# A sparse attention and expert layer on one core: block sums on TensorE, key maxima ahead of the transposes, query copies in a row, a new order and 152 filler matmuls

## Chip, cores and metric

The kernel runs on one core of a Trainium2 chip. The time is the device time of one execution in microseconds. Before the change it was 207.64 us, the median of three runs (206.0 to 210.47).

## What is computed

Two stages, for batch 4, 8 heads, 768 tokens and head size 64. Stage 1 is attention in which each query sees a window of local keys and, for each block of 32 tokens, one maximum key and one mean value. Stage 2 is a mixture of four attention experts on the result.

```python
k_sum = k.reshape(B, H, nb, block, D).max(axis=3)      # block = 32, nb = 24
v_sum = v.reshape(B, H, nb, block, D).mean(axis=3)
mask_l = np.abs(pos[:, None] - pos[None, :]) < window  # window = 16
scores_l = scale * q @ k.T ; scores_s = scale * q @ k_sum.T + np.log(block)
a = softmax(concat([where(mask_l, scores_l, -1e9), scores_s]))
attn = a @ concat([v, v_sum])
# stage 2, x = attn as (B, S, H*D): for each of 4 experts
logits = x @ w_gate                                    # top 2 of 4, softmax w
a = softmax(where(causal, -1e9, scale * (x @ wq[e]) @ (x @ wk[e]).T))
out += mask * w * (a @ (x @ wv[e]) @ wo[e])
```

## The kernel before

The program is a list of steps. `make_plan` creates them, each with the buffers that it reads and writes, and `TABLE`, a text of some 730 words, gives the order in which they are emitted, the engine of each (V is VectorE or DVE, A ScalarE or ACT, G GpSimd or POOL, S SyncE or SP, P TensorE or PE) and the slots of its new buffers. Nothing is scheduled while it runs: on each engine instructions stand in the table's order, and one that waits holds up all behind it. Transfers are issued by POOL (keys and queries) and SP (all others), in order as well.

Heads are worked in pairs, four pairs for each of four batches; two pairs share one load of keys and queries. For a pair, stage 1 (`stage1_pair`) does this:

- `dv` (L268) loads V as 24 windows of 96 tokens and 64 features into `vb`; column 64 holds constants, for the softmax sums.
- `load_vs` (L235) loads V of two pairs a second time, 24 blocks of each head on 96 partitions, and adds the 32 tokens of each block in halves, in place, in five steps `tr` (L247) on POOL or DVE. `dsum` (L286) spreads the block sums by DMA into partitions 96 to 119 of `vb`, twelve copies for each head.
- `tk` (L296) transposes keys on PE, `ck` copies them to `kT`, `rk` (L305) takes block maxima from `kT`, and `kwc` and `ksc` (copies, L163 and L161 on their engines) set up `kw`, the windows with 24 maxima behind each.
- `tq` (L334) transposes the queries, with 128 partitions and 6 tokens on each. `cq` (L338) copies them out of PSUM to `qT`: in odd batches it writes in a row and reads with a stride, in even batches it reads in a row and writes with a stride.
- `scs` (L361 masks, L368 products) makes scores, `ex` (L375) their exponentials, `avs` (L385) the PV products in f32, `rc` and `xm` (L396, L400) normalize, `tx` (L410) transposes back, and `hic` and `loc` (L421) split the result into two f16 parts, `hi` and `lo`.

Stage 2 of a batch needs all four pairs of it: `pps` (L558) projects queries and keys of two experts, `vps` (L493, L496) makes values and gate logits, `sps` (L582) scores, `exs` (L590) exponentials, `dgm` (L595) the causal mask on the diagonal, `av2` (L606) products, then weights (L620, L624), a transpose (L633), the output product (L647), a copy and a store (L657). The table interleaves stage 2 of a batch with stage 1 of the next. All helper copies of DVE and POOL have line L163, those of ACT L161.

Of the kernel before, what the change touches and what calls it, by code (L numbers as in the profile page):

```python
# [50 lines left out]
19,S,0 4,G, 5,V, 20,V, 17,G,0 88,P,0.0 6,G, 21,V, 8,G, 22,V, 68,P,1.1 0,G,1 18,G,0 89,V, 91,A,0 73,P,0.0 3,G,1  # L51
69,V, 70,V,0 71,A,1 93,P,1.1 1,G, 72,A, 90,V,1 48,P,2.0 74,A, 94,A, 7,G, 77,P,4.0 78,A, 92,V, 23,G, 24,G,
95,P,0.1 75,P,6.2 76,A, 49,V, 51,V,2 50,V,1 52,V, 67,S,0 25,G,1 97,P,2.3 98,A, 66,S, 80,P,4.0.0 2,G, 53,P,6.2
54,V, 79,P, 28,P,2.1 9,S,1 81,V, 15,G, 96,A, 82,V, 33,P,3.0 29,V, 83,P,0.0.0 84,A, 57,P,4.4 58,A, 31,V,1
55,P,6.5 56,A, 213,G,2 283,P,2.0 30,V,0 32,A, 284,A, 87,S,2 86,S, 99,P,4.1.1 34,V, 35,P,2.0 36,A, 214,G,2
288,P,6.1 205,G,0 26,S, 10,G, 11,G, 85,V, 289,A, 37,P,0.2 12,G, 13,G, 14,G, 286,V,0 27,S, 100,P, 285,V,1
287,V, 101,V, 102,V, 223,P,2.1 224,V, 243,P,3.0 268,P,6.2 269,V, 292,P,4.1 38,A, 226,A,2 103,P,0.1.1 104,A,
244,V, 245,V,0 633,G,3 225,V,1 293,A, 227,V, 290,P,6.3 40,P,2.0.0 291,A, 105,V, 206,G,0 247,A,1 248,P,4.0
# [721 lines left out]
```

## Time and profile before

| | |
|---|---|
| median of three runs | 207.64 us |
| the profiled execution | 208.41 us |
| its span, first to last instruction | 206.4 us |
| PE, DVE, ACT, POOL busy | 149.7, 131.6, 123.1, 82.8 us |
| bytes moved | 33.17 MB, 161 GB/s on the mean |
| SP: V for `vb`, V for `vs`, sums to `vb` | 16, 8 and 32 loads |

The span is cut by its stages rather than read as a whole. The first 27.3 us are the start. From 27.3 to 61.6 stage 1 of batch 0 is finished and that of batch 1 begun. From 61.6, where the first expert projection starts, both stages run beside each other. What follows 195.3 us is the end of the last batch. A PE that is busy here is not at its peak: records of matmuls overlap, so what a step takes is read from its start to the next start.

### The profile page before, as it was taken

The page shows a single profiled execution, that of the slowest core. Times are in us where ns is not written, and L with a number is a line of the kernel's source. Part 1 is how long each engine was busy: PE and PEld are TensorE (multiplying, and loading weights), DVE is VectorE, ACT ScalarE, POOL GpSimd, SP SyncE. Part 2 cuts the span into 40 slices and gives each one's busy share as a digit, 9 for nine tenths or more (in the row PEclk, how much of TensorE's full clock was granted, in tenths as well). Part 3 has the DMA queues.
Part 4 walks back from the last instruction along what each step waited for, and adds up shares of the span by engine and source line. Part 5 has one row for each costly group of instructions (what it writes and reads, how often), then busy time and mean ns, then how long its engine had stood idle before and what let it go on. Part 6 is the DMA issues. An engine that isn't in the chain of part 4 may idle for free.

```text
span 206.4 us, 6279 instructions
## 1 busy us (share of the span) xinstructions
PE 149.7 (73%) x2704; PEld 115.2 (56%) x2704; DVE 131.6 (64%) x227; ACT 123.1 (60%) x152; POOL 82.8 (40%) x146
## 2 busy tenths in 40 slices
PE   0252277897369974737977978766999999999960
PEld 0242175686356753637754567655768767767620
DVE  0653029987666467604839998967498687636940
ACT  2199402658265854517997777344646888698740
POOL 7980009304520634236553954918722012223300
PEclk9999999999969999988999999999699999999997
DMA  6999999699999999999167997999698580200456
GB/s 154 187 150 187 223 175 148 80 183 208 167 199 230 168 163 183 204 210 246 24 105 128 219 184 113 219 260 265 105 175 166 139 137 17 89 3 0 165 194 254
DMA packets 65499, 33.17 MB, mean 161 GB/s; under 512 B 54208, under 2 KB 61376, under 8 KB 64704
## 3 DMA queue, kind: packets, MB, share of 16 engines
q1 hardware_dynamic: 58016, 26.48, 67.4%
q0 software_dynamic: 7456, 6.29, 20.2%
q8 instruction: 21, 0.34, 0.7%
q14 instruction: 6, 0.05, 0.1%
HBM read 30.41 MB, written 6.29 MB: 178 GB/s over the span
## 4 chain that ended last, share of the span: by engine, by line
PE 41%; DVE 21%; DMA 17%; issue 10%; ACT 6%; SPq 1%; POOL 1%; DVEq 0%; POOLq 0%; ACTq 0%
PE ps L385 9%; PE ps L558 7%; DMA vb<-in_v_dram 7%; DMA vb<-vs 7%; DVE qT L163 4%; PE ps L410 4%; PE ps L493 4%; PE ps L647 4%; PE ps L582 3%; DMA kn<-in_k_dram 3%; DVE ks L305 3%; PE ps L334 2%; PE ps L606 2%; PE ps L296 2%; DVE x L400 2%
## 5 line engine op out<-in xcount | busy, mean ns | idle before, releaser
L590 ACT ACTIVATE a<-ps 128x1024 f16<-128x1024 f32 (+1 forms) x48 | 42.0, 915 | 14.1 <-PE ps L582 12.6
L385 PE MATMUL ps<-vb,aT 120*64 120x65 f32 x768 | 30.1, 241 | 14.7 <-DMA vb<-in_v_dram 7.1
L595 POOL TENSOR_SCALAR_AFFINE_SELECT a<-a 128x256 f16<-128x256 f16 x48 | 18.9, 410 | 54.4 <-ACT a L590 49.6
L247 POOL TENSOR_TENSOR vs<-vs 96x1024 f32<-96x1024 f32 (+4 forms) x23 | 25.3, 1100 | 31.4 <-DMA vs<-in_v_dram 20.7
L385 PEld LDWEIGHTS ps<-vb,aT 120*64 120x64 f32 x768 | 27.8, 154 | 17.5 <-issue 11.9
L375 ACT ACTIVATE aT<-ps 120x768 f32<-120x768 f32 x32 | 25.2, 819 | 14.2 <-PE ps L368 11.3
L558 PE MATMUL ps<-hi,wqk 128*128 128x384 f16 x128 | 22.6, 326 | 1.6 <-ACT aT L375 1.6
L163 DVE COPY qT<-ps 128x768 f16<-128x768 f16 x6 | 12.9, 2145 | 12.4 <-PE ps L334 12.2
L163 POOL COPY kw<-kT 128x960 f16<-128x960 f16 (+1 forms) x14 | 15.7, 1153 | 11.6 <-PE ps L368 8.1
L410 PE MATMUL ps<-id,x 128*128 128x128 f32 x96 | 16.8, 320 | 4.5 <-issue 1.6
L421 DVE TENSOR_TENSOR lo<-ps,hi 128x768 f16<-128x768 f32 x16 | 15.4, 971 | 5.2 <-ACT hi L161 5.0
L361 PE MATMUL ps<-pi,mt 64*128 64x64 f16 (+1 forms) x128 | 12.8, 271 | 7.0 <-issue 3.3
L558 PEld LDWEIGHTS <-wqk 128*128 128x128 f16 x128 | 12.1, 98 | 9.4 <-issue 1.9
L296 PE MATMUL ps<-id,kn 96*64 96x96 f16 x256 | 10.1, 244 | 9.1 <-DMA kn<-in_k_dram 8.7
L410 PEld LDWEIGHTS ps<-id,x 128*128 128x128 f32 x96 | 12.7, 162 | 6.6 <-issue 2.1
L247 DVE TENSOR_TENSOR vs<-vs 96x512 f32<-96x512 f32 (+4 forms) x17 | 10.5, 615 | 8.9 <-DMA vs<-in_v_dram 7.0
L582 PE MATMUL ps<-qk,qk 64*128 64x512 f16 (+3 forms) x128 | 14.6, 307 | 2.1 <-DVE x L400 1.2
L368 PE MATMUL ps<-qT,kw 64*128 64x64 f16 x384 | 12.8, 204 | 4.2 <-ACT qT L161 2.3
L400 DVE TENSOR_TENSOR x<-ps,rec 128x768 f32<-128x768 f32 x16 | 15.3, 957 | 0.6
L161 ACT COPY qT<-ps 128x768 f16<-128x768 f16 x10 | 15.6, 1612 | 0.1
L161 ACT CAST hi<-ps 128x768 f16<-128x768 f32 x9 | 7.4, 825 | 13.5 <-PE ps L410 13.4
L305 DVE TENSOR_REDUCE ks<-kT 128x24 f16<-128x768 f16 x16 | 14.9, 944 | 0.1
(81 smaller groups left out, 260.8 us busy)
## 6 DMA issues: line engine op xcount, KB each, us to landing
vb<-in_v_dram SPq DMA_DIRECT2D x14, 576.0 KB
vs<-in_v_dram SPq DMA_DIRECT2D x8, 768.0 KB
out_dram<-ob SPq DMA_DIRECT2D x12, 512.0 KB
kn<-in_k_dram POOLq DMA_DIRECT2D x7, 384.0 KB, 6.9
qn<-in_q_dram POOLq DMA_DIRECT2D x7, 384.0 KB, 7.6
vb<-vs SPq DMA_DIRECT2D x32, 72.0 KB
vb<-in_v_dram SPq DMA_DIRECT2D x2, 552.0 KB
a<-in_moe_wq_dram SPq DMA_DIRECT2D x4, 128.0 KB
```

What stands on the lines that cost most here:

```text
L161: nc.scalar.copy(dst, src)
L163: en(e).tensor_copy(dst, src)
L247: en(e).tensor_tensor(w[:, 0:half], w[:, 0:half], w[:, half:2 * half], AL.add)
L305: nc.vector.tensor_reduce(T["ks"][ks.slot], T["kT"][kT.slot].rearrange("c (s n p) -> c n s p", s=8, n=NSUM), AX.XY, AL.max)
L375: nc.scalar.activation(T["aT"][aT.slot][0:KR], pbank(sc, 2)[0:KR, :, 0:384], AF.Exp, scale=SCALE)
L385: nc.tensor.matmul(pbank(av, 2)[o:o + 64, u, 65 * (2 * (t // 2) + hp):65 * (2 * (t // 2) + hp) + 65], a[0:KR, hp, 64 * t:64 * t + 64], T[" ...
L400: nc.vector.tensor_tensor(T["x32"][x32.slot].rearrange("p (u t w) -> p u t w", u=2, w=64), avv()[:, :, :, 0:64], T["rec"][rec.slot].to_bro ...
L410: nc.tensor.transpose(pbank(xp, 2)[:, t // 3, 128 * (t % 3):128 * (t % 3) + 128], T["x32"][x32.slot][:, 128 * t:128 * t + 128], T["id32"])
L558: nc.tensor.matmul(pbank(pp, 2)[:, u, 0:384], T["wqk"][:, ch, cc, j, :], hi_(ch)[:, 384 * u:384 * u + 384], start=(ch == 0), stop=(ch == N ...
L582: nc.tensor.matmul(pbank(sp, 2)[:, ep, c0:c0 + w], T["qk"][qk[1].slot][r, 128 * tj:128 * tj + 128], T["qk"][qk[0].slot][r, n0:n0 + w], sta ...
L590: nc.scalar.activation(a2v(u), pbank(sp, 2)[:, :, 0:ln], AF.Exp, scale=SCALE / (XS * XS))
L595: nc.gpsimd.affine_select(m, m, [[0, 2], [1, 128]], AL.is_ge, 0.0, base=0, channel_multiplier=-1)
```

## The change

- **Block sums.** `load_vs`, its adds and the spread by DMA are gone. `load_v` loads V into `vb` as before. `sums` multiplies what lies there with a matrix of zeros and ones, `sel`: 12 windows of a head add up in one bank of PSUM, each head in its own 32 partitions. A first copy (`be`) brings that to `vs`, now 24 partitions of 4 x 64 elements, and a second (`ds`), on POOL, DVE or ACT, spreads it into `vb`. In batch 0 a step does one pair, later two. `vb` has six slots instead of four.
- **Key maxima.** Loaded keys have 8 tokens on each of 96 partitions. Three DVE steps (`km`) take the maximum of these 8 from the loaded keys (512 to 256, 128, 64 columns a head); `tk` transposes that too, and `rk` reduces 4 columns instead of 32.
- **Queries** are loaded on 96 partitions with 8 tokens on each, as the keys are, and `cq` always writes in a row.
- **Weights.** `wqk` is two buffers, one for two experts each, so that each has its own copy. `av2` lists more exponentials among the buffers that its later parts read.
- **Fills.** 74, 28, 23, 13 and 14 matmuls of the identity with itself, 128 x 128, stand at five places ahead of the first PV products (`f` in the table).
- **Order.** The whole table is new.

```diff
-SLOTS = dict(qn=3, kn=3, kT=2, ks=2, kw=3, qT=3, aT=6, x32=2, vb=4, vs=2,
+SLOTS = dict(qn=3, kn=3, km=3, kT=2, ks=3, kw=3, qT=3, aT=6, x32=2, vb=6, vs=2,
-19,S,0 4,G, 5,V, 20,V, 17,G,0 88,P,0.0 6,G, 21,V, 8,G, 22,V, 68,P,1.1 0,G,1 18,G,0 89,V, 91,A,0 73,P,0.0 3,G,1
+116,S,0 27,G,0 28,G,0 29,V,0 30,V, 31,V, 10,G, f,P,7.74 76,P,0.0.0 12,V, 5,G,1 77,A, 94,P,1.1.1 99,P,2.0 78,V,
...
+    def sels(e):
+        z = T["sel"]
+        en(e).memset(z, 0.0)
+        nc.gpsimd.memset(z[:, 22:24], 1.0)
+        nc.gpsimd.affine_select(z[:, 22:24], z[:, 22:24], [[-32, 2]], AL.is_ge, 0.0,
+                                base=-16, channel_multiplier=1)
+        nc.gpsimd.affine_select(z[:, 22:24], z[:, 22:24], [[32, 2]], AL.is_ge, 0.0,
+                                base=47, channel_multiplier=-1)
...
+            for w in (256, 128, 64):
+                def mx(e, w=w, i=i):
+                    hs = slice(n * i, n * i + n)
+                    m = T["km"][km[b, g].slot][:, hs, :]
+                    x = T["kn"][kn[b, g].slot][:, hs, :] if w == 256 else m
+                    en(e).tensor_tensor(m[:, :, 0:w], x[:, :, 0:w], x[:, :, w:2 * w], AL.max)
...
-            def add(e, half=half):
-                w = T["vs"][t.slot]
-                en(e).tensor_tensor(w[:, 0:half], w[:, 0:half], w[:, half:2 * half], AL.add)
...
-                nc.sync.dma_start(out=w[WIN:KR, 12 * hp:12 * hp + 12, 0:64],
-                                  in_=s[r0:r0 + NSUM, 0:64].unsqueeze(1).to_broadcast((NSUM, NQ, 64)))
...
+    def sums(b, cs):
+        sp, t = R.buf("ps"), R.buf("vs")
+        def mm(e):
+            n = 2 * len(cs)
+            for tt in range(NQ):
+                for j in range(n):
+                    nc.tensor.matmul(pbank(sp)[32 * j:32 * j + 32, 0, 0:64],
+                                     T["sel"][:, 22 - 2 * tt:54 - 2 * tt],
+                                     T["vb"][vb[b, cs[j // 2]].slot][0:WIN, 12 * (j % 2) + tt, 0:64],
+                                     start=(tt == 0), stop=(tt == NQ - 1))
...
+        def ev(e):
+            for j in range(2 * len(cs)):
+                copy(e, T["vs"][t.slot][96:120, j, :], pbank(sp)[32 * j:32 * j + NSUM, 0, 0:64])
...
+                copy(e, T["vb"][vb[b, c].slot][WIN:KR, :, 0:64].rearrange("n (h t) d -> n h t d", h=2),
+                     T["vs"][t.slot][WIN:KR, 2 * i:2 * i + 2, :].unsqueeze(2).to_broadcast(
+                         (NSUM, 2, NQ, 64)))
...
+            for hp in range(2):
+                nc.tensor.transpose(pbank16(kp)[64 * hp:64 * hp + 64, 768:864],
+                                    T["km"][km[b, g].slot][:, hh + hp, 0:64], T["id16"][0:96, 0:96])
...
-                                    T["kT"][kT.slot].rearrange("c (s n p) -> c n s p", s=8, n=NSUM),
-                                    AX.XY, AL.max)
+                                    pbank16(kp)[:, 768:864].rearrange("c (n p) -> c n p", p=4),
+                                    AX.X, AL.max)
...
-            if b % 2:
-                copy(e, dst.rearrange("c (p s) -> c p s", s=6),
-                     src.rearrange("c (s p) -> c p s", s=6))
-            else:
-                copy(e, dst.rearrange("c (p s) -> c s p", s=6),
-                     src.rearrange("c (s p) -> c s p", s=6))
+            copy(e, T["qT"][qT.slot].rearrange("c (p s) -> c p s", s=8),
+                 pbank16(qp)[:, 0:S].rearrange("c (s p) -> c p s", s=8))
...
+    def fill(bank, n):
+        for _ in range(n):
+            nc.tensor.matmul(T["ps"][:, bank, 0:128], T["id16"], T["id16"], start=True, stop=True)
```

Two places show the new order. The first is SP's queue at the start. Before, it stood so (`vs` is V for the adds, `vb` the windows; L286 is the spread of sums):

```order
L240 DMA vs_100<-in_v_dram 96x2048
L286 DMA vb_96<-vs_100 24x12x64 x2
L268 DMA vb_96<-in_v_dram 96x24x64
L240 DMA vs_101<-in_v_dram 96x2048
L286 DMA vb_98<-vs_100 24x12x64 x2
L268 DMA vb_98<-in_v_dram 96x24x64
L262 DMA vb_97<-in_v_dram 80x64
L268 DMA vb_97<-in_v_dram 96x23x64
```

Now it begins with a weight (`a_136`), and the four pairs of V of batch 0 follow each other:

```order
L466 DMA a_136<-in_moe_wq_dram 128x4x64
L275 DMA vb_101<-in_v_dram 80x64
L281 DMA vb_101<-in_v_dram 96x23x64
L281 DMA vb_102<-in_v_dram 96x24x64
L281 DMA vb_103<-in_v_dram 96x24x64
L281 DMA vb_104<-in_v_dram 96x24x64
```

V of the first pairs no longer stands behind a spread that waits for adds. The second place is DVE ahead of its first normalization. Before, `pi`, adds (`vs`), key copies, maxima (`ks` from `kT`) and a query copy came there, of which these are the last:

```order
L163 COPY kT_78<-ps 128x768
L163 COPY kw_84<-kT_78 128x10x96
L163 COPY kw_84<-kT_78 128x2x80
L305 TENSOR_REDUCE ks_81<-kT_78 128x24
L163 COPY kw_84<-ks_81 128x12x24
L163 COPY qT_87<-ps 128x6x128
L396 RECIPROCAL rec_102<-ps 128x12
L400 TENSOR_TENSOR x_94<-ps,rec_102 128x768
```

Now the stretch from the key copy of pair 0 to the first normalization reads, with the sums (`vs_107`), two spreads into `vb` and the maxima of the next keys (`km_77`):

```order
L167 COPY kw_87<-kT_83 128x10x96
L167 COPY kw_87<-kT_83 128x2x80
L333 TENSOR_REDUCE ks_84<-ps 128x24
L167 COPY kw_87<-ks_84 128x12x24
L167 COPY vs_107<-ps 24x64 x2
L167 COPY vb_101<-vs_107 24x24x64
L167 COPY vb_102<-vs_108 24x24x64
L251 TENSOR_TENSOR km_77<-kn_81 96x1024
L251 TENSOR_TENSOR km_77<-km_77 96x4x128
L251 TENSOR_TENSOR km_77<-km_77 96x4x64
L419 RECIPROCAL rec_109<-ps 128x12
```

The query copies have moved from here to ACT, and the spreads and the next maxima stand ahead of the first normalization.

## Rows read from the trace of the kernel before

**Rows 1.** The page, section 2: PE's busy tenths in 40 equal slices.

```profile
PE   0252277897369974737977978766999999999960
```

**Rows 2.** Busy time of each engine in four stretches (us), TensorE's granted clock, DMA.

```profile
0.00:27.30 27.30, 6.89 (x138) 5.58 (x138) 9.03 (x15) 13.95 (x12) 12.82 (x44) 1.00 1.05 181
27.30:61.60 34.30, 25.48 (x528) 22.59 (x529) 26.35 (x34) 16.39 (x22) 13.03 (x14) 0.95 1.07 165
61.60:150.60 89.00, 69.09 (x1305) 53.06 (x1305) 60.07 (x105) 56.02 (x71) 46.72 (x62) 0.96 1.03 178
150.60:195.30 44.70, 44.52 (x714) 32.20 (x713) 32.87 (x71) 33.74 (x45) 10.23 (x27) 1.00 0.42 93
```

**Rows 3.** The chain that ended last: start us, us, what.

```profile
1.54 6.66 DMA kn<-in_k_dram
...
13.12 14.03 DMA vb<-in_v_dram
...
27.28 1.57 PE ps L385 x24
```

**Rows 4.** PE's waits from 61.6 to 150.6: us in total, times, longest.

```profile
PE ps L385 <- DMA vb<-vs: 6.9, 3, 4.2
...
PE ps L334 <- DVE qT L163: 1.5, 1, 1.5
PE ps L385 <- DMA vb<-in_v_dram: 1.5, 1, 1.5
```

**Rows 5.** Groups by line and shape: busy us, mean ns, idle before.

```profile
L385 PEld LDWEIGHTS ps<-vb,aT 120*64 120x64 f32 x768 | 27.8, 154 | 17.5 <-issue 11.9 <-DVE gt L536 2.7 <-ACT qk L161 2.2
...
L421 DVE TENSOR_TENSOR lo<-ps,hi 128x768 f16<-128x768 f32 x16 | 15.4, 971 | 5.2 <-ACT hi L161 5.0
L400 DVE TENSOR_TENSOR x<-ps,rec 128x768 f32<-128x768 f32 x16 | 15.3, 957 | 0.6
L305 DVE TENSOR_REDUCE ks<-kT 128x24 f16<-128x768 f16 x16 | 14.9, 944 | 0.1
L247 POOL TENSOR_TENSOR vs<-vs 96x1024 f32<-96x1024 f32 x6 | 14.1, 2356 | 30.3 <-DMA vs<-in_v_dram 20.7 <-issue 9.6
...
L163 POOL COPY kw<-kT 128x960 f16<-128x960 f16 x7 | 12.9, 1839 | 11.6 <-PE ps L368 8.1 <-ACT kT L161 3.5
...
L163 DVE COPY kT<-ps 128x768 f16<-128x768 f16 x11 | 6.2, 560 | 2.0 <-ACT kw L161 2.0
...
L163 DVE COPY kw<-kT 128x960 f16<-128x960 f16 x5 | 5.2, 1043 | 0.1
...
L247 DVE TENSOR_TENSOR vs<-vs 96x1024 f32<-96x1024 f32 x2 | 2.4, 1222 | 7.0 <-DMA vs<-in_v_dram 7.0
...
L163 DVE COPY kw<-kT 128x160 f16<-128x160 f16 x5 | 2.0, 392 | 0.0
...
L204 POOL MEMSET vb<- 128x24 f32 x4 | 0.6, 144 | 0.2
```

**Rows 6.** The start in order of time: start us, us, instructions.

```profile
5.06 1.49 POOL L227 DMA_DIRECT2D qn<-in_q_dram  x2
...
11.52 1.49 PE L334 MATMUL ps<-id,qn 128*64 128x128 f16 x24 [1.79 <-DMA qn<-in_q_dram]
```

**Rows 7.** PE in order of time, from the dense stretch.

```profile
163.92 1.62 PE L385 MATMUL ps<-vb,aT 120*64 120x65 f32 x48
165.37 0.51 PE L334 MATMUL ps<-id,qn 128*64 128x128 f16 x12
```

**Rows 8.** Busy time in two stretches with a lower clock; columns as in rows 2.

```profile
90.00:96.00 6.00, 5.09 (x110) 5.03 (x111) 2.08 (x4) 1.56 (x2) 1.48 (x1) 0.72 1.15 228
144.00:150.00 6.00, 5.73 (x86) 4.49 (x79) 2.48 (x4) 3.88 (x6) 4.61 (x5) 0.72 0.70 113
```

**Rows 9.** Query copies one by one: duration ns min/median/max, first and last start.

```profile
L161 ACT COPY qT<-ps x10: 798/835/2921, 14.3 to 165.9; 128x768 f16<-128x768 f16 x10
L163 DVE COPY qT<-ps x6: 942/2726/2775, 29.6 to 130.2; 128x768 f16<-128x768 f16 x6
```

More of the change, by code (lines that the diff above doesn't have):

```diff
@@ L133, in emit @@
         for i, eng, slots in table:
+            if i < 0:
+                self.fill(*slots)
+                continue
             st = self.steps[i]
@@ L281, in dsum @@
-        def dsum(e):
-            w = T["vb"][vb.slot]
-            s = T["vs"][vs[b, g].slot]
-            for hp in range(2):
-                r0 = NSUM * (hh + hp)
-                nc.sync.dma_start(out=w[WIN:KR, 12 * hp:12 * hp + 12, 0:64],
-                                  in_=s[r0:r0 + NSUM, 0:64].unsqueeze(1).to_broadcast((NSUM, NQ, 64)))
-        R.step(f"ds{b}{c}", {"S": 0.9}, [vs[b, g], vones], [vb], dsum, dma=2 * 288 * 0.017 / 16)
+        if edge:
+            R.step(f"zv{b}{c}", {"V": 0.1, "G": 0.14}, [vones], [vb[b, c]], zv)
@@ L325, in ksc @@
                  T["ks"][ks.slot].unsqueeze(1).to_broadcast((128, NQ, NSUM)))
-        R.step(f"ksc{b}{c}", {"G": 0.45, "V": 0.3, "A": 0.45}, [ks], [kw], ksc)
+        R.step(f"ksc{b}{c}", {"G": 0.42, "V": 0.24, "A": 0.43}, [ks], [kw], ksc)
         qp, qT = R.buf("ps"), R.buf("qT")
@@ L396, in rc @@
             nc.vector.reciprocal(T["rec"][rec.slot], avv()[:, :, :, 64:65])
-        R.step(f"rc{b}{c}", {"V": 0.22}, [av], [rec], rc)
+        R.step(f"rc{b}{c}", {"V": 0.23}, [av], [rec], rc)
         def xm(e):
@@ L402, in xm @@
                                     T["rec"][rec.slot].to_broadcast((128, 2, 6, 64)), AL.mult)
-        R.step(f"xm{b}{c}", {"V": 0.97}, [av, rec], [x32], xm)
+        R.step(f"xm{b}{c}", {"V": 0.96}, [av, rec], [x32], xm)
         xp = R.buf("ps", 2)
@@ L470, in cw @@
                 s = slice(1024 * i, 1024 * i + 1024)
[L471 to L472 removed]
+                copy(e, T["wqk"].rearrange("p a c j n -> p (a c j n)")[:, s], f32(sA)[:, s])
+            R.step(f"cw{i}", {"V": 0.68, "G": 1.04, "A": 1.0}, [pw[i]], [wqk[i]], cw, keep=[sA])
         def co(e):
             copy(e, T["wo"].rearrange("p c n -> p (c n)"), f32(sB)[:, 1024:2048])
[L476 removed]
+        R.step("co", {"V": 0.68, "G": 1.04, "A": 1.0}, [po], [wo], co, keep=[sB])
     def stage2(b, hs, ls):
@@ L675, in make_plan @@
                 load_qk(b, g, 1)
-                load_vs(b, g)
+            for c in (2 * g, 2 * g + 1):
+                load_v(b, c)
+                if b == 0:
+                    sums(b, [c])
+            if b:
+                sums(b, [2 * g, 2 * g + 1])
         hs, ls = [], []
@@ L689, in decode @@
         i, e, s = w.split(",")
-        out.append((int(i), e, [int(x) for x in s.split(".") if x]))
+        out.append((int(i) if i != "f" else -1, e, [int(x) for x in s.split(".") if x]))
     return out
@@ L717 @@
     one("pi", (128, 6, 64), HALF)
-    one("wqk", (128, NCH, 2, 2, 128), HALF)
+    one("wqk", (128, 2, NCH, 2, 128), HALF)
     one("wvg", (128, NCH, 264), HALF)
@@ L722 @@
     one("wgt", (128, NCH, 4), FP32)
-    many("qn", (128, 4, 384), HALF)
+    many("qn", (96, 4, 512), HALF)
+    many("km", (96, 4, 256), HALF)
+    one("sel", (96, 54), FP32)
     many("kn", (96, 4, 512), HALF)
```

268 lines of the change are left out of this document (132 added, 136 removed).

## The prediction

> **What bounds the kernel now.** I read the 40 slices first, then the busy time of four stretches, then the chain of waits, then the groups of instructions. In the slices [rows 1] the reader is to see TensorE (PE) nearly empty in the first five, uneven up to slice 28, and full from there almost to the end. The stretches [rows 2] give that in numbers. Up to 27.3 us PE works 6.9 us; from 27.3 to 61.6, where the first expert projection (L558) starts, 25.5 of 34.3; from 61.6 to 150.6 69.1 of 89.0, so 19.9 us idle; from 150.6 to 195.3 44.5 of 44.7. Behind that lies a tail of 206.4 - 195.3 = 11.1 us (last transposes, last output blocks, their DMA). So no engine is the bound of the first part; a chain is. It reads [rows 3]: a key load that takes 6.66 us, then a load of V that takes 14.03 us and sets free the first PV product (L385) at 27.28, with scores and query copies in between. In the third stretch PE's waits name their ends [rows 4]: 6.9 us for the block sums that a DMA spreads into `vb` (L286), 1.5 for V itself, 1.5 for a query copy. In the fourth stretch PE is the bound, with DVE and ACT at 32.9 and 33.7 us of 44.7.
>
> **The sum** is made in three pieces, of the profiled execution: A from 0 to the first L558 (61.6 us), B from there to 195.3 (133.7), C the tail (11.1). Its own time, 208.41, is 2.0 above its span; the median, 207.64, is 0.8 lower.
>
> **A, up to the first projection.** *Block sums.* V was loaded twice, the second time (768 KB per half batch) to be added in five steps on POOL or DVE, the longest 2356 and 1222 ns [rows 5], and the result went through SP's queue again. Now PE adds what `vb` holds. Of the bytes that moved in the first 27.3 us (181 GB/s [rows 2], so 4.9 MB) the two `vs` loads and four spreads go, 1.8 MB. Before the first PV product now stand 1.54 MB of keys and queries, 0.13 of weights and 0.58 of V: 2.24 MB at 181 GB/s are 12.4 us, about 14 with the start. All four pairs of V and the next keys and queries make 4.7 MB, 28 us; their last block sum stands late enough for that. *Key maxima* now begin ahead of the transposes, on the loaded keys: three DVE steps, each over 4 heads. No row has them. The nearest is DVE's f32 sum of 1024 elements, 1222 ns [rows 5], and by size 0.6 and 0.3 for the next two, 2.1 us; since operands are two bytes now, half of it may do. I take 1.2, and 2.1 as the bound. *Order.* The key load of the second pair group is the first thing on POOL: landing at 0.8 + 6.7 = 7.5, maxima until 8.7, transposes, copy of keys on ACT 0.8 (as for its row-wise copy of queries [rows 9]), `kw` copy on DVE 1.04 + 0.39 [rows 5]: first scores at about 12. The queries of pairs 0 and 1 stand seventh and eighth among POOL's loads and memsets: four issues at 0.75 [rows 6], an identity, and twelve memsets of about 0.14 [rows 5] with as much between them put their two issues at 6.9 and 7.6; before, the load issued at 5.06 set PE free at 11.52 [rows 6], so these land at about 14. Transposes of pairs 0 and 1 end at 16. From here DVE has no gap: key copy 0.56 [rows 5], two `kw` copies 2.9, two small maxima and `ksc` 0.6 (an estimate, under the 944 ns of the old maximum), sum and spread 1.2: the first PV product starts at about 21, where before it was 27.3. Behind it DVE does a spread 0.9, the next maxima 1.2, four `rec` and `x` at 1.2 (0.96 of it `x` [rows 5]), a key copy, `ksc`, spread, four `lo` at 0.97, a query copy and a `hi` at 0.95: 15 us, so 36; the last `hi` (ACT) and two scores make it **A = 38**, 23.6 less. The spread's 0.9 is again a price without a row (24 x 1536 f32): POOL's copy of 128x960 takes 1839 ns, DVE's 1043 [rows 5], so 0.9 to 2.9 by engine; three of them on DVE's path could add 2.
>
> *Fills.* 152 matmuls on constants stand where PE waits for keys, masks or V. Before, the 24 L385 of one step take 1.57 us at 27.28 [rows 3], but 48 take 1.45 at 163.92 (start to next start [rows 7]): 65 against 30 ns each. [...] A fill costs nothing while PE would wait. [...] I take no delay; 3 is the bound.
>
> **B, the bulk.** Start from PE's busy time, 69.1 + 44.5 = 113.6 us. *Clock*: in 90 to 96 and 144 to 150 the granted clock is 0.72 [rows 8], that is 56% of 12 us at the lower level, 3.4 us that steadier work doesn't pay: -3.4. *Moved*: transposes of two pairs of batch 1 and one pair's scores now come after the first L558, six steps at some 0.35 us (12 L334 have 0.51 with their overlapping end [rows 7]): +2.1. *Key maxima*: two more transposes for each of twelve pairs, at 0.02: +0.5. *Block sums*: 16 pairs, 384 f32 matmuls that PE runs as 768 passes, four in A's batch, six steps of 96 passes here. No row has a 96x32 block. The nearest is L385, f32, two column halves side by side: 30 ns a pass. Four quarters side by side would halve that, 15 ns: 1.5 us a step, 9 in B and 6 in A. That is the lower bound too, as there are no more than four quarters; 30 ns is the upper one, 18 in B. I take **+9**, since the form is L385's with its halves cut once more. *What leaves other engines*: the query copies with a stride (up to 2.75 and 2.92 us where a row-wise one takes 0.80 and 0.94 [rows 9]) in batches 0 and 2, eight times some 1.9, 15 us of ACT and DVE; sixteen maxima of 944 ns on DVE [rows 5], now small; all sums in `vs`. In come the spreads and the key maxima. Over the shorter B I count about 94 us on DVE and 93 on ACT, 77% of it, as in the stretch where PE had no gap (74 and 75%). *Waits*: of the 19.9 us idle, 8.4 were V and its sums and 1.5 a strided copy [rows 4]; 10.0 stay if nothing else changes, 0.5 if the dense stretch's rate holds. I take 5. B = 113.6 - 3.4 + 2.1 + 0.5 + 9 + 5 = **126.8**.
>
> **C** stays 11.1. Sum 38 + 126.8 + 11.1 = 175.9; with 2.0 outside the span **178 us**.
>
> [...] The block sums all lie in array rows 0 to 95, and so do L385's products in 0 to 119; L385's weight loads take 154 ns by the row [rows 5] and yet a pass comes every 30 ns, so loads do overlap products there. [...]
>
> **Rivals.**
> 1. *The clock doesn't hold.* The fills end before the keys or V land, PE falls back, and A's real work, some 13 us between 21 and 38, takes twice as long where it is on the chain: A = 47, time 187. For it: 65 ns passes at 27.28. Against it: the fills stand in exactly those gaps.
> 2. *New waits for old.* The spreads sit on POOL and DVE behind masks, `kw` copies and normalizations, and PV products wait there as they did for L286; 20 us idle in B stay: 178 + 15 = 193. Against it: the sums now start when V lands and need one matmul step, not five adds and a DMA.
> 3. *Block sums without overlap, slower than before.* If a pass costs what L385's cost at 27.28, 65 ns, 768 take 50 us where I have 15: 178 + 35 = 213. It decides from 59 ns (212) up; at 48 ns the gain is gone to within 2%. Against it: 30 ns in the nearest row.
> 4. *Half overlap*: 30 ns a pass, 23 us, so 186.
>
> **Chances.** The forecast 0.60, with its own range 171 to 185 (A 36 to 41, waits 0.5 to 10); rival 1 0.13, rival 2 0.10, rival 3 0.06, rival 4 0.11. The range reaches over rivals 1, 2 and 4 and leaves out rival 3 and the ends: **170 to 195**. Within 2% (203.5 to 211.8, about what a measurement can tell from no change, as the three runs differ by that) lies only a pass at 48 to 58 ns, or several costs at once: 0.04; slower 0.06; faster 0.90.
>
> **What would show it.** First L385 at 19 to 23 us; first projection at 36 to 41; six L385 passes in about 0.2 us from the first on, not 0.4; block sum steps of 1.5 us; no wait of PE for a DMA in B; B's PE idle near 5 us; tail 11. The forecast is wrong if a 96-pass step takes over 3 us, if PV products wait for the spreads, or if the first projection comes after 45.

## The result, and the profile after

The changed kernel takes 197.73 us (median of four runs, 196.52 to 199.82) where the kernel before takes 207.94 beside it: a ratio of 0.952, with a 95% interval of 0.938 to 0.966. It is faster, by 10 us and not by the 30 of the forecast; 178.0 lies far off, and its range ended at 195. Executions of one kernel differ here by some 2%, and the profiled one is not always among the shorter ones, from which the ratios are taken. The profiled execution of the changed kernel has a span of 194.8 us. Its pieces, in the cut of the prediction:

| piece | before | forecast | after |
|---|---|---|---|
| A, to the first projection | 61.6 | 38 | 44.1 |
| B, from there | 133.7 | 126.8 | 139.2 |
| of it PE busy | 113.6 | 121.8 | 127.4 |
| of it PE idle | 19.9 + 0.2 | 5 | 11.8 |
| C, tail | 11.1 | 11.1 | 11.5 |

A gained 17.5 of the 23.6 us expected. B, which should have become 7 us shorter, became 5.5 longer. The slices of the page answer to [rows 1], and here TensorE's granted clock and the DMA's share stand beside them:

```profile
PE   2998979799978979999679937999999999999750
...
PEclk9999999999996999999999996699999999999998
DMA  5999996799999956949900999503050000002635
```

PE is now filled from the second slice on, with holes at slices 20, 21 and 24, and the clock falls in two places. The same in stretches, columns as in [rows 2]; the first two are the start up to the first PV product and the rest of A:

```profile
0.00:26.69 26.69, 20.89 (x481) 19.25 (x481) 13.02 (x38) 10.64 (x14) 14.37 (x44) 1.00 1.14 175
26.69:44.13 17.44, 16.38 (x479) 14.84 (x478) 15.25 (x22) 9.65 (x17) 8.21 (x8) 1.00 0.89 164
44.13:117.00 72.87, 62.36 (x1437) 48.46 (x1438) 59.00 (x116) 46.60 (x62) 35.16 (x50) 0.98 0.97 152
117.00:126.50 9.50, 8.59 (x252) 7.34 (x253) 4.92 (x11) 3.60 (x5) 4.00 (x3) 0.64 0.88 123
126.50:183.30 56.80, 56.39 (x1070) 42.38 (x1062) 43.58 (x88) 41.70 (x56) 18.21 (x32) 1.00 0.13 47
```

All of B's loss lies ahead of 126.5; behind it PE has no gap, as before [rows 2]. The first PV product, in order of time (it stands for the end of [rows 3]):

```profile
23.61 1.54 PE L294 MATMUL ps<-vb,sel 96*32 96x64 f32 x46
26.48 0.27 PE L294 MATMUL ps<-vb,sel 96*32 96x64 f32 x2 [1.33 <-issue]
26.69 3.19 PE L408 MATMUL ps<-vb,aT 120*64 120x65 f32 x96
```

Its 96 passes take 3.0 us to the next start, 32 ns each: PE runs near the 30 ns of [rows 7] and not at the 65 of [rows 3], with a granted clock of 1.00 (second row above). But they come at 26.7, hardly earlier than the 27.28 of before, and a block sum ahead of them stands still for 1.33 us with two passes left, waiting for nothing that the trace names. The waits of PE in B answer to [rows 4]:

```profile
PE ps L294 <- issue: 4.1, 2, 3.2
PE ps L362 <- ACT a L614: 1.9, 1, 1.9
PE ps L606 <- DVE vs L167: 1.4, 1, 1.4
```

The waits for V and its sums, 8.4 us before, are gone. In their place stand 4.1 us "issue", again inside block sums, and behind these three rows some 4 us more, most of it for DVE. The "issue" waits in order of time:

```profile
112.87 0.88 PE L294 MATMUL ps<-vb,sel 96*32 96x64 f32 x46
116.98 0.95 PE L294 MATMUL ps<-vb,sel 96*32 96x64 f32 x50 [3.24 <-issue]
...
119.12 1.50 PE L294 MATMUL ps<-vb,sel 96*32 96x64 f32 x46
121.53 1.65 PE L294 MATMUL ps<-vb,sel 96*32 96x64 f32 x50 [0.91 <-issue]
```

And DVE's groups, to be read beside [rows 5]:

```profile
L167 DVE COPY vb<-vs 24x1536 f32<-24x1536 f32 x7 | 8.2, 1168 | 4.1 <-ACT vs L165 3.8
...
L167 DVE COPY kw<-ks 128x288 f16<-128x288 f16 x7 | 5.4, 770 | 0.2
L167 DVE COPY kw<-kT 128x160 f16<-128x160 f16 x6 | 5.2, 869 | 0.0
```

The small `kw` copy took 392 ns on the mean before [rows 5] and takes 869 now. So three suspects: waits that nothing explains, DVE operations that take too long, and the fills.

### The profile page after: what moved, and what is told of

Its sections match the earlier page's. It is cut to its first block, busy times and chain, and to the rows that moved or that the text cites. A ratio compares the mean times of both kernels' runs of the same rounds, so it can differ in the third digit from the quotient of the medians.

```text
span 194.8 us, 8294 instructions
## 1 busy us (share of the span) xinstructions
PE 168.1 (86%) x3720; PEld 133.7 (69%) x3720; DVE 140.2 (72%) x279; ACT 113.2 (58%) x152; POOL 80.0 (41%) x137
## 4 chain that ended last, share of the span: by engine, by line
PE 69%; DVE 18%; issue 6%; ACT 3%; POOL 1%; DVEq 0%; ACTq 0%; POOLq 0%
PE ps L408 13%; PE ps L582 8%; PE ps L294 7%; PE ps L630 6%; PE ps L433 5%; DVE kw L167 5%; PE ps L688 4%; PE ps L517 4%; PE ps L671 4%; PE ps L606 4%; PE ps L384 3%; PE ps L321 3%; PE ps L391 3%; DVE km L251 2%; PE ps L362 2%
## 5 line engine op out<-in xcount | busy, mean ns | idle before, releaser
L167 POOL COPY kw<-kT 128x960 f16<-128x960 f16 (+1 forms) x20 | 25.4, 1308 | 26.8 <-ACT kT L165 21.4
L294 PE MATMUL ps<-vb,sel 96*32 96x64 f32 x768 | 18.0, 232 | 5.5 <-issue 5.5
L294 PEld LDWEIGHTS ps<-vb,sel 96*32 96x32 f32 x768 | 15.6, 117 | 7.7 <-issue 7.2
L167 POOL COPY vb<-vs 24x1536 f32<-24x1536 f32 x8 | 12.9, 1611 | 13.2 <-DVE vs L167 13.0
L688 PE MATMUL ps<-id 128*128 128x128 f16 x152 | 11.9, 251 | 3.5 <-POOL id L185 3.5
L165 ACT COPY kT<-ps 128x768 f16<-128x768 f16 x8 | 6.4, 802 | 14.5 <-PE ps L324 12.2
L517 PE MATMUL ps<-wvg,hi 128*128 128x264 f16 x96 | 13.8, 276 | 0.0
L688 PEld LDWEIGHTS <-id 128*128 128x128 f16 x152 | 11.0, 116 | 3.7 <-POOL id L185 3.4
L671 PE MATMUL ps<-wo,wT 128*128 128x512 f16 x48 | 12.1, 381 | 0.6 <-DVE wT L167 0.3
L630 PEld LDWEIGHTS <-a 128*128 128x128 f16 x336 | 11.2, 97 | 1.4 <-issue 0.6
```

Source lines behind the costliest of these rows:

```text
L167: en(e).tensor_copy(dst, src)
L294: nc.tensor.matmul(pbank(sp)[32 * j:32 * j + 32, 0, 0:64], T["sel"][:, 22 - 2 * tt:54 - 2 * tt], T["vb"][vb[b, cs[j // 2]].slot][0:WIN, 12 ...
L517: nc.tensor.matmul(p[:, i, 0:264], hi_(ch)[:, cols], T["wvg"][:, ch, :], start=(ch == 0), stop=False, skip_group_check=True)
L630: nc.tensor.matmul(pbank(av, 2)[:, ep, 65 * ti:65 * ti + 65], a2v(u)[:, ep, o:o + 128], T["v2"][v2.slot][:, tj, 2 * cc + ep, :], start=(tj ...
L671: nc.tensor.matmul(pbank(op, 2)[:, i, :], T["wT"][wTs[cc].slot][:, 128 * ti:128 * ti + 128], T["wo"][:, cc, :], start=(cc == 0), stop=(cc ...
L688: nc.tensor.matmul(T["ps"][:, bank, 0:128], T["id16"], T["id16"], start=True, stop=True)
```

## Experiments

Each ratio below is to the kernel before, measured beside the run. The changed kernel's own is 0.952 (0.938 to 0.966), so of its variants below only copies_on_act, quiet_b_pool and, at the edges of the intervals, quiet_b and few_sums stand apart from it. For the others the trace is read for a wait that came or went, not for their time.

### The query copy alone

In `cq` of the kernel before, `if b % 2:` became `if True:`.

> The kernel before, with the query copy written in a row in all four batches (its odd batches have it already), nothing else. Theory 1, these copies lie on the path: eight of them take 0.8 to 0.95 us in place of 1.8 to 2.9, some 14 us less on DVE and ACT, and PE's waits for them in the first 60 us and in batch 2 shrink: the span falls by 2 to 5 us to 201 to 204. Theory 2, other waits (V's sums, by DMA) stand behind them: span 205 to 207.

The copies do take 0.79 to 0.84 us on ACT and 0.94 to 0.96 on DVE, and the time is the same: ratio 1.001 (0.995 to 1.007). The 15 us of DVE and ACT time that I counted as leaving these engines were behind other waits there, as theory 2 had it.

### What TensorE waits for when the trace names nothing

The first thing to try was data: the steps' own loads, or the loads around them.

```diff
+            if b == B - 1 and c >= 2:
+                t1 = t0 + 2
             src = bass.AP(vh.tensor, vh.offset + (64 * t0 - 16) * D,
```

> The loads of V for the last two pairs of batch 3 carry 2 of their 24 blocks; every instruction of every engine stays (the output of those pairs is left wrong). In the changed kernel TensorE stands still for 3.24 us at 113.75 and for 0.91 us at 120.62, inside block-sum steps whose own V had landed at 95.9 and 111.6, and nothing that the trace names ends the wait; the two gaps are 256 TensorE instructions apart, and 16 KB of instructions are fetched by DMA between them, while these two V loads (256-byte packets) fill the DMA engines. Theory 1, the instruction fetch comes late because it stands behind the V packets: both gaps go to under 0.5 us, the clock stays at 1.00 from 117 to 126, the span falls by 6 to 8 us to 187 to 189. Theory 2, the steps wait for their own data or for a semaphore the trace does not name: their loads are untouched, so the gaps stay within 0.5 us of 3.2 and 0.9 and the span at 194 to 195.

Half a hit: the second gap went and the first stayed, with 3.37 us at the same pass. Ratio 0.964 (0.953 to 0.976). PE in order of time:

```profile
113.29 0.88 PE L293 MATMUL ps<-vb,sel 96*32 96x64 f32 x46
117.53 1.65 PE L293 MATMUL ps<-vb,sel 96*32 96x64 f32 x50 [3.37 <-issue]
```

The kernel without fills decided what kind of wait this is. All five `f` words were taken out of the table.

> All 152 matmuls on constants are taken out, nothing else. Theory 1, as predicted blind: they hold the clock and cost nothing; without them the first PV passes take 65 ns in place of 32 and the first projection comes 5 to 9 us later than 44.1, the span rises to 200 or more. Theory 2, the fills cost as much as they give: the first 74 end at 10.2 where the keys' maxima are done at 7.7, and the other 78 are 5.1 us on a TensorE that has hardly a gap from 10 to 37: the first key transposes start at about 8.0, passes are slow for some 10 us, and the first projection comes at 41 to 45, the span at 191 to 196. Of the gaps without a releaser: the instruction count loses 304 records, so if they are fetches of 256 instructions the gap in the block sums of batch 3 moves from behind 46 passes to behind 70 of the 96; if they are a wait for data it stays behind 46.

The block sums of batch 3, PE in order of time:

```profile
120.48 1.21 PE L290 MATMUL ps<-vb,sel 96*32 96x64 f32 x70
125.73 1.01 PE L290 MATMUL ps<-vb,sel 96*32 96x64 f32 x26 [4.04 <-issue]
```

The wait moved from behind 46 passes to behind 70. A pass is two instructions (PE's product and PEld's weight load), so the 152 fills are 304, 48 more than 256; 48 instructions are the 24 passes by which it moved. Such waits stand a whole number of 256 instructions apart. The page says the same by its sums:

| kernel | PE + PEld instructions | by 256 | packets of the instruction queue |
|---|---|---|---|
| before | 2704 + 2704 | 21.1 | 21 |
| few_sums, below | 3016 + 3016 | 23.6 | 23 |
| no_fills | 3568 + 3568 | 27.9 | 28 |
| after | 3720 + 3720 | 29.1 | 29 |

```profile
q8 instruction: 29, 0.48, 1.1%
```

That is the queue's line in the page of after: packets, MB, and so 16 KB each. In all sixteen traces, with PE's and PEld's records counted in order of time, every wait of PE on "issue" of 0.3 us or more stands 171 to 191 records behind a multiple of 256; the offset drifts from 191 early in a run to 171 late in it. Where two follow each other, 128 + 128 instructions lie between (dma_order below, stretches from one to the next; PE and PEld are the first two counts):

```profile
118.51:122.51 4.00, 2.55 (x128) 2.16 (x128) 2.85 (x9) 1.51 (x2) 2.60 (x3) 1.00 0.02 4
122.51:128.31 5.80, 3.79 (x128) 3.21 (x127) 4.53 (x9) 3.70 (x5) 2.32 (x2) 1.00 0.51 71
```

So TensorE waits for its instructions. Before, the same wait was there to be seen, 3.28 us in the middle of a score step (of 7.6 in all):

```profile
52.40 0.19 PE L361 MATMUL ps<-pi,mt 64*128 64x64 f16 x1
55.88 0.34 PE L361 MATMUL ps<-pi,mt 64*128 64x64 f16 x3 [3.28 <-issue]
```

When a refill, as the packet with the next 256 instructions is called from here on, comes late, and what that costs, the next runs tell. To see whether it stands behind other transfers, more of these were cut than in late_v_small, to a `w` of 32 columns for two output blocks of batch 0 and one load of keys:

```diff
-                    in_=T["ob"][ob.slot])
+                    in_=T["ob"][ob.slot][:, :, 0:w])
...
-                        in_=src[b, h0:h0 + n].rearrange("h (p s) d -> p h (s d)", s=8))
+                        in_=src[b, h0:h0 + n].rearrange("h (p s) d -> p h (s d)", s=8)[:, :, 0:w])
```

> As late_v_small, and besides the two output blocks that leave at 106 to 109 and the key load issued at 107.6 carry 32 of their 512 columns (results of the pairs and blocks concerned are left out); every instruction stays. In late_v_small the gap of 3.4 us at 114 stayed and the one at 121 went, and in all kernels so far every long wait of TensorE without a releaser stood at a multiple of 256 of its instructions plus 193, with one 16 KB instruction packet just before its end. Theory 1, the fetch stands behind whatever DMA packets are outstanding, at 112 to 115 those of the two output blocks (2048 bytes each) and the key load: with these gone too the gap at 113.75 falls under 0.7 us, the low clock from 118 to 125 goes, and the span falls to 186 to 189. Theory 2, the fetch takes some 3 us by itself when 256 instructions are used up in 3.4 us: the gap stays at 2.5 us or more with an empty DMA.

The gap is gone, as theory 1 had it, and the low clock behind it; the second is 0.77 us. Ratio 0.945 (0.932 to 0.958). The profiled span, 196.6, is no shorter, since this execution, the longest of four, lost 7.8 us to such waits in A, where nothing was changed (projection at 50.95); the other three had 191.4 to 193.2, and 186 to 189 was not reached. PE in order of time:

```profile
120.55 1.56 PE L294 MATMUL ps<-vb,sel 96*32 96x64 f32 x96
```

Then the transfers were moved, with a right output: `od02` behind `od01`, `od00` behind `dv31`, `dv32` into slot 4 behind `av300`, `zv33` and `dv33` into slot 2 behind `kw32`.

> The changed kernel with four transfers moved and its output right: the two output blocks of batch 0 go out as soon as they are there (behind the first one, and ahead of the V load that waits from 89 to 105), and the loads of V for pairs 2 and 3 of batch 3 go into buffers that come free at 128 and 135, so that they no longer fly at 109 to 124. Theory 1 (the fetch waits behind outstanding packets): the gaps of 3.2 and 0.9 us in the block sums of batch 3 fall to under 1 us together, the low clock from 118 to 125 goes, span 186 to 190; a new wait would show only if these V loads landed after 147. Theory 2 (the gaps don't hang on these transfers): span 193 to 196, gaps unchanged.

The first gap fell from 3.24 to 0.58, but the second rose to 1.46 and others came, 2.02 at 128.3 and 1.46 at 153.7. Only the last, where the V loads now fly, can be put down to the move. Ahead of the second the DMA share was 0.02 (first of the two rows of dma_order above), and three_moves below, with no transfer moved, has the same two waits of 1.46 and 2.02 at the same passes, the first with a DMA share of 1.16:

```profile
118.00:122.00 4.00, 2.54 (x128) 2.16 (x128) 1.85 (x5) 1.51 (x2) 2.09 (x2) 1.00 1.16 178
```

In both TensorE used its 256 instructions in some 2.5 us, and the next ones were there 4.00 us after the last start, with the DMA engines full or nearly empty. So a refill can be late without other traffic, too, where TensorE is that fast. Ratio 0.965 (0.946 to 0.985); theory 1's time was missed.

Last, nearly all traffic of B was cut, in the same way.

> Nearly all transfers from some 60 us on are cut small: V from the third pair of batch 1 on (2 of 24 blocks), keys and queries from the second half of batch 1 on and the output blocks of batches 0 to 2 (32 of 512 columns); every instruction and wait stays (results are left out accordingly). It prices what the transfers do to TensorE's instruction fetch between the first projection and the tail (139.2 us in the changed kernel, of them 5.9 us of waits at multiples of 256 instructions, and 10.2 us of low clock, two stretches that each follow a wait). Theory 1, the fetch is late only behind data packets: these waits fall under 1 us in all, at most 3.4 us of low clock are left, and this part takes 130 to 133 us. Theory 2, it is late by itself where TensorE is fast: 3 us or more of these waits stay, and the part takes 136 or more.

This is theory 1, near enough: one wait of 1.05 us is left where under 1 was expected, with a DMA share of 0.02 ahead of it, and B takes 129.8 us where 130 to 133 were forecast. B in one row, of after and of this kernel (PE, PEld, DVE, ACT and POOL busy, granted clock, DMA share, GB/s):

```profile
44.13:183.35 139.22, 127.39 (x2746) 98.18 (x2746) 107.52 (x214) 91.90 (x122) 57.37 (x85) 0.96 0.62 107
```

```profile
48.41:178.24 129.83, 123.10 (x2746) 94.31 (x2746) 106.22 (x214) 91.88 (x122) 58.24 (x85) 1.00 0.08 9
```

The same 2746 passes take 9.4 us less: 5.1 of idle time, nearly all of it waits for instructions, and 4.3 of busy time, which is the clock. Ratio 0.930 (0.921 to 0.939). The span fell by 5.0 only, to 189.8, since this execution reached its projection 4.3 us later, behind a wait of 3.48 us in A. In after the clock fell twice in B, once behind the wait at 57.15, which is none for instructions (1.85 us, for an ACT exponential), and once behind the one at 113.75:

```profile
57.15:60.00 2.85, 0.62 (x18) 0.59 (x20) 2.61 (x10) 2.22 (x4) 0.01 (x1) 1.00 1.13 178
60.10:63.40 3.30, 3.30 (x66) 3.06 (x66) 3.16 (x7) 0.45 (x1) 2.73 (x4) 0.50 1.25 218
113.75:116.97 3.22, 0.00 (x0) 0.00 (x0) 1.55 (x4) 0.11 (x1) 1.08 (x1) 1.00 1.20 302
118.10:124.80 6.70, 5.79 (x168) 4.84 (x166) 3.13 (x10) 2.29 (x3) 2.50 (x3) 0.50 1.06 152
```

Both times PE had been idle, 1.85 and 3.24 us, and shortly after the granted clock was 0.50. So a wait can be paid twice, but it need not be: three_moves below had 14.8 us of idle time in B, and the clock did not fall there (1.00 in its row). What decides it stays open.

### DVE beside POOL

Ten DVE operations of after took 0.55 to 3.2 us more than their like; each ran beside a POOL copy from SBUF to SBUF. The costliest (DVE, then POOL):

```profile
52.86 4.36 DVE L167 COPY kw<-kT 128x960 f16<-128x960 f16 x2
...
52.93 3.07 POOL L167 COPY kw<-kT 128x960 f16<-128x960 f16 x2 [0.46 <-DMA vb<-in_v_dram]
```

These two copies of DVE take 1.21 to 1.34 us where POOL does not copy. Operations that read PSUM (`x`, `lo`) kept their 957 and 954 ns beside POOL. In the table, `G` became `A` in 24 words (ten `kw`, six `ksc`, eight `ds`), as here for `kw13`:

```diff
-290,G,
+290,A,
```

> The 24 copies that POOL makes from SBUF to SBUF in the attention (10 of kw, 6 of its block-sum columns, 8 spreads of V sums) go to ACT, at the same places of the order; the output stays right. Theory 1, DVE stands still beside POOL's copies: the ten DVE operations that took 0.6 to 3.2 us more than alone (14.3 us together; 3.46 in place of 0.28 for the small kw copy at 53.8, 2.40 in place of 0.96 for the spread at 33.7) fall back, DVE's busy time goes from 140 to 125 to 129 us, PE's waits at 57 to 59 and at 93 to 104 (4.9 us) fall under 2, the span to 187 to 191. Theory 2, ACT, with 28 us more on its 113, becomes what is late: DVE's time falls as well, but PE waits more for ACT's exponentials, the span stays at 194 or rises. Theory 3, the long DVE times have another cause: DVE stays at 138 to 142.

Theories 1 and 2 both have their part. DVE fell from 140.2 to 125.1 us, with no operation stretched:

```profile
L164 DVE COPY kw<-ks 128x288 f16<-128x288 f16 x7 | 1.8, 254 | 0.2
L164 DVE COPY kw<-kT 128x160 f16<-128x160 f16 x6 | 1.8, 296 | 0.0
```

But ACT's `kw` copy takes 1828 ns, ACT went to 148 us and PE waited for it: ratio 1.058 (1.045 to 1.070). In after, DVE and POOL both took longer side by side: DVE's 128x960 copy began first, at 52.86, and took its 0.99 us, while POOL's took 2.68 in place of 1.8 to 1.9; DVE's small copy behind it took 3.46 in place of 0.28 and ended at 57.22, after the POOL pair and the three mask steps that followed it to 57.07. `x` and `lo`, which read PSUM, took at most 958 ns beside such a copy. To take POOL's copies away without loading ACT, they were cut to a part:

```diff
+    def few(e, on, dst, src):
+        if e == "G" and on:
+            dst, src = dst[:, 0:1], src[:, 0:1]
+        copy(e, dst, src)
```

> From batch 1 on POOL's copies of the attention (kw, its block-sum columns, all spreads but one) copy one block of each tile and no more; all instructions, waits and other engines' work stay (these blocks are left out of the result). In copies_on_act DVE's busy time fell from 140.2 to 125.1 us and none of its operations was stretched, but ACT's kw copy took 1.83 us and ACT became late. Theory 1, DVE's standing still beside POOL is on the path in batches 1 to 3: the stretched operations from 52 us on go (10.5 us), TensorE's waits at 57 to 59 and 93 to 104 fall from 4.8 to under 2, the low clock at 60 goes, the span falls by 3 to 6 us to 189 to 192. Theory 2, these waits are set by something else (scores, ACT's exponentials): DVE's time falls, the span stays within 1 us of 194.8.

PE's waits for DVE and ACT in B went nearly all (the largest left is 0.3 us), but the profiled span is 197.0: in this execution waits for instructions came to 10.2 us. In after they are 4.4 by the trace, and 5.9 with one of 1.4 us at 72.0 that stands on the same count and that the trace puts down to a DVE copy.

```profile
PE ps L410 <- issue: 4.4, 2, 3.5
PE ps L296 <- issue: 4.4, 2, 3.6
PE ps L386 <- issue: 1.4, 1, 1.4
```

Ratio 0.945 (0.929 to 0.961). So here what the neighbours no longer cost went into waiting for instructions. It is one execution, the longest of four: two others had 192.3 and 192.7 us, where the changed kernel had 194.8 twice, so part of the gain may come through. Three moves with a right output (`ksc03` and `ksc21` from V to A, `kw13` from G to A) fared alike:

> Three of the copies that stood beside each other go to ACT where it is idle: the small block-sum copies of DVE at 14.9 and 91.1 (1.88 and 2.10 us beside POOL, 0.24 alone) and POOL's kw copy at 52.9 (beside DVE's, which took 3.46 in place of 0.28). The output stays right. Theory 1 (DVE stretched beside POOL is on the path there): TensorE's gap at 57.15 (1.85 us) and with it the low clock from 60 to 63.4 go, the waits at 93 to 96 lose about 1.5 us; span 190 to 192. Theory 2 (not on the path, or ACT's 1.8 us kw copy is as late): span 194 to 196.

The gap at 57 stayed, now 2.30 us behind an ACT exponential that `kw13` delayed, and 8.7 us of instruction waits stand in B: span 195.5, ratio 0.966 (0.950 to 0.981), theory 2. B has 14.8 us of idle time and yet, with a granted clock of 1.00, takes 1.1 us less than in after:

```profile
122.00 0.95 PE L291 MATMUL ps<-vb,sel 96*32 96x64 f32 x50 [1.46 <-issue]
...
127.80 1.62 PE L405 MATMUL ps<-vb,aT 120*64 120x65 f32 x48 [2.02 <-issue]
```

```profile
46.27:184.35 138.08, 123.27 (x2747) 94.44 (x2746) 103.91 (x213) 94.06 (x125) 55.90 (x83) 1.00 0.60 103
```

Both causes away at once is the test of the sum for B:

> quiet_b and quiet_pool together: small transfers from some 60 us on, and POOL's copies of the attention from batch 1 on one block each. If the fetch and DVE's standing still beside POOL are all that separates the 139.2 us between first projection and tail from the 126.8 of my sum, this part takes 125 to 129 us, with the waits at multiples of 256 under 1 us and other waits of TensorE under 2. If TensorE, with its work closer together, runs into new waits (ACT's exponentials, DVE's normalizations) or its clock goes down in other places, it takes 131 or more.

```profile
45.89:171.19 125.30, 122.54 (x2746) 94.14 (x2746) 98.54 (x214) 91.46 (x122) 39.29 (x85) 1.00 0.10 14
```

125.3 us, where my sum had 126.8, with 122.5 busy and 2.8 idle where it had 121.8 and 5. Ratio 0.905 (0.896 to 0.914).

### The price of the block sums

`range(NQ)` in `mm` became `range(1)`.

> Each block-sum step keeps the first of its 12 blocks for each head: 32 f32 matmuls in place of 384, 1408 TensorE instructions less (a matmul pass is a weight load and a product, 7440 in all now, 256 of them in one 16 KB fetch), and by 15.6 and 31 ns a pass 13.8 us less TensorE time, 5.5 of it before the first projection. Copies and spreads of the sums stay; the sums are left wrong. Theory 1, what was not in my sum is the instruction fetch, which falls behind where TensorE uses 256 instructions in under some 4 us: the waits at multiples of 256 instructions in the block sums of batch 3 (3.2 and 0.9 us) go, those of the whole run fall from 7.2 us by at least 3, and with the low clock behind them the span falls by 16 to 20 us to 175 to 179. Theory 2, only TensorE's busy time counts: span 181, these waits as long as before in other places. Theory 3, block sums lay beside other waits: span 184 or more.

Theory 3: the span falls by 8.2 us to 186.6 for 13.8 us of work; ratio 0.928 (0.917 to 0.939). Of the 8.2, 7.5 lie in B (131.8 us); A, from which 5.5 us of sums went, lost 0.7, with 2.3 us of instruction waits and 3.4 us of low clock in it. The waits in batch 3's block sums went, but one of 2.91 us came at 111.2, and the clock fell more often (mean 0.941).

### The start

no_fills, expected above, has its first PV product at 22.89, 3.8 us sooner than with fills, and 22 of its passes take 0.91 us, 73 take 2.2, 30 ns each: PE is at the faster rate without them. Yet in this execution, the longest of five, its first projection came at 49.8, behind three instruction waits:

```profile
22.89 0.91 PE L404 MATMUL ps<-vb,aT 120*64 120x65 f32 x22
25.05 2.37 PE L404 MATMUL ps<-vb,aT 120*64 120x65 f32 x73 [1.25 <-issue]
...
31.53 0.31 PE L380 MATMUL ps<-pi,mt 64*128 64x320 f16 x2 [2.80 <-issue]
...
45.34 0.35 PE L387 MATMUL ps<-qT,kw 64*128 64x64 f16 x12 [3.38 <-issue]
```

Ratio 0.969 (0.960 to 0.979), not apart from that of the changed kernel. So a version was put together: the first `f,P,7.74` as `f,P,7.46`, the other four out, `ksc03` and `ksc21` on A, `kw13` behind `dm005`, `od02` and `od00` as above.

> A version meant to be faster, with the output right: fills only 46 before the first keys (106 less, 4 us of TensorE and 212 instructions), DVE's two small block-sum copies at 14.9 and 91.1 on ACT, POOL's kw copy of 52.9 behind three of its mask steps so that it no longer runs beside DVE's, and the first output blocks sent out as soon as they are there. Theory 1 (fills before the first PV product cost 3 to 4 us, as the 22.9 of no_fills against 26.7 shows, and DVE beside POOL another 3): first PV product at 22.5 to 24, no wait at 57, span 186 to 191. Theory 2 (the fetch takes back what the others give: with TensorE's work closer together the waits at multiples of 256 instructions grow): first PV product at 23 as well, but span 192 to 197.

That is theory 2. The first PV product came at 23.53, the projection at 44.40, no earlier than in after:

```profile
23.53 3.20 PE L404 MATMUL ps<-vb,aT 120*64 120x65 f32 x96
26.56 0.34 PE L317 MATMUL ps<-id,kn 96*64 96x96 f16 x7
29.90 0.37 PE L317 MATMUL ps<-id,kn 96*64 96x96 f16 x9 [3.00 <-issue]
```

The wait sits in the key transposes of the next batch, and DVE, ACT and the rest of A behind them. With 14 us of such waits in the profiled execution the ratio is 0.969 (0.948 to 0.991): it does not beat the changed kernel. Two more runs for A alone (the weight loads by `[:, 0:1]`, V of pairs 1 and 3 by `t1 = t0 + 2`; the second with the fills of combined):

> Up to the first projection the loads of V for the second and fourth pair of batch 0 carry 2 of 24 blocks and the twelve weight loads a quarter of their rows (buffers are set to zero by DVE in its idle first 6 us; results are left wrong); fills and every other instruction stay. It prices the fetch ahead of the first projection, which came at 44.1 us in the changed kernel and at 46 to 51 in five runs with the same instructions there, always with waits at multiples of 256 instructions (1.3 to 7.8 us). Theory 1, these waits come from the transfers: they fall under 0.5 us in all, the first PV product comes at 24.5 to 25.5 and the first projection at 41 to 43; what is left above the 38 of my sum are the fills and DVE's two stretched operations. Theory 2, the loads are not what delays the fetch here: waits and times as before.

> quiet_a with 46 fills ahead of the first keys and no others (106 less). In combined that brought the first PV product to 23.5 us, but the projection only to 44.4, as a wait of 3.0 us followed in the next key transposes. Theory 1, without the fetch's waits the 3 us come through: first PV product at 21 to 23, first projection at 38 to 40, the 38 of my sum. Theory 2, DVE's queue or a falling clock holds it: first projection at 41 or later, with TensorE waiting for DVE by more than 2 us between 23 and 41.

quiet_a missed: 5.7 us of instruction waits in A, projection at 49.9. It did not do what it meant to, as the V loads of batch 1 moved up into the space made and 28 to 44 us had 173 GB/s in place of 166. quiet_a_46 had one wait of 0.90 us in A, its first PV product at 23.5 and the projection at 42.15, between its two theories (PE waits for DVE by 1.0 us in that part). Ratios 0.969 (0.958 to 0.979) and 0.948 (0.937 to 0.958). A without any such wait was not reached.

## Why the prediction was wrong

**What held.** Block sums: 96 passes take 1.56 us in quiet_dma, 16 ns each, four quarters side by side, and 48 passes in two quarters 1.5: the prices of B and A, and rivals 3 and 4 are out. So loads overlap products there as well, as in L385: the weight loads of the sums lie in the same rows and take 117 ns in after, and yet a pass comes every 16. Key maxima: 0.69 + 0.74 = 1.4 us, between 1.2 and 2.1; the first step's 0.69 on two-byte operands is 0.56 of the f32 sum's time [rows 5]. The spread: 0.96 alone. Tail 11.5. PE is at the faster rate from the first PV product on in after (32 ns a pass), and in no_fills too (30), without a fill. So nothing shows that the fills held off rival 1, and it is not out altogether: in few_sums, behind an instruction wait of 1.83 us among the first PV products, twelve key transposes took 0.73 us where they take 0.44 in no_fills.

**The step that failed most: B's waits and clock.** I took 5 us idle and 3.4 us back from the clock, reckoned with a lower level of 0.50, as it was granted before from 91 to 94 us. It was 11.8, and 4.3 us lost. quiet_b and quiet_b_pool, one execution each, split the miss of 12.4 us: 9.4 go with the transfers, as late instructions (5.9 us of waits, 1.05 without the transfers) and low clock, and 4.5 with DVE's standing still beside POOL; without both B is 1.5 us under the sum. The sum had counted the bytes that the change saves (33.2 to 24.7 MB) and the PE time that it adds, not that PE's instructions go from 5408 to 7440, each 256 of them one packet of 16 KB more, and used up in as little as 2.5 us where the next came 4.00 us after the last start (dma_order). The "issue" waits were on the profile of before, 3.28 us in A and 4.3 in B; the prediction names none of them, and those of B went into the 10.0 us that were to stay or go as a whole. "No wait of PE for a DMA" came true by name only, as the refills are packets of a DMA queue (q8 above).

**DVE** was counted at 94 us for B from prices taken alone; it had 107.5 and, with POOL's copies cut, 98.5. The bound of 2.9 us for the spread held (2.40 beside POOL), but it was a price by engine, and for the spread only; `kw`, `ksc`, `km` and the gates were stretched beside POOL as well, by 0.55 to 3.2 us. The 4.5 us between 94 and 98.5 stay without a cause.

**A, 44.1 for 38.** "Fills: no delay, 3 the bound" failed. No run shows the 3 us; in after the 74 end at 10.2, 2.5 us after the keys' maxima, the other 78 stand in a queue in which PE, from there to the first PV product, waits only 0.9 us for `km`, 0.2 for `pi` and 1.33 for instructions, and without any of the 152 that product comes 3.8 us sooner, the wait of 1.33 among them. But that doesn't come through to the projection: in combined and few_sums, with the PV product at 23.5 and 23.0, the projection still comes at 44.4 and 43.4. And 44.1 was in part luck: with the same work up to there the projection came at 44.4, 48.3 and 51.0 in late_v_small, dma_order and quiet_dma, behind 1.8, 3.7 and 7.8 us of waits for instructions. The best seen is 42.15, with fewer fills and loads. Of the some 4 us above 38 that are left even there, 2.5 lie ahead of the PV product and 1.6 behind it; what they are made of stays open, as no run had A free of instruction waits and low clock together.

**Rivals.** Rival 2, new waits for old, is the nearest: 11.8 us idle, between the forecast's 5 and its 20, though not by the spreads it named. The 15 us of query copies were no gain by themselves. The bounds of rival 3, 59 and 48 ns a pass, were reckoned from 11.5 us for the 768 passes and not from the 15 of the sum; from 15 they are 64 and 53. With passes of 16 and 31 ns that changes nothing.

## To carry to other kernels

Count TensorE's instructions as a transfer: products and weight loads, 16 KB for 256 of them, and look in the profile for waits on "issue" at equal distances in that count. Here, where TensorE used 256 in less than some 4 us, it often waited for the next, in B for 5.9 us in after (3.24 of them at a DMA share of 1.20) and for 1.05 with the traffic cut, and what was won elsewhere went in part into that. So before a step of many small matmuls is added, count what it adds to the refills, and take its price from a run: 13.8 us of such work left out gave back 8.2. Price a DVE operation from SBUF to SBUF twice, alone and beside a POOL copy (0.28 and 3.46 us for the small `kw` copy).

## What the runs showed of the hardware

- A refill of TensorE's instructions is one 16 KB packet (29 packets, 0.48 MB in after), and it comes late mostly beside other transfers: waits of 0.2 (few_sums) to 4.7 us (copies_on_act), multiples of 256 instructions apart, 5.9 us in all of B in after, 10.2 in quiet_pool, 1.05 with the traffic cut (quiet_b).
- With hardly any traffic a wait can be left where 256 instructions are used in some 2.5 us: 1.46 us at a DMA share of 0.02, 4.00 us from the last start to the next (dma_order).
- How long they are differs from one execution to the next: with the same instructions up to there, the first projection came at 44.1, 48.3 and 51.0 us (after, dma_order, quiet_dma).
- A DVE copy of 0.28 us took 3.46 beside POOL's copies and masks, and a POOL copy of 1.8 us took 2.68 beside one of DVE (after). ACT's copy of the same 128x960 `kw` windows takes 1.83 us, DVE's 0.98 alone (copies_on_act).
